# Writing the halves of q into the place of the loaded q, four buffers for split p, and new ranks for the planner

## The chip, the cores and the metric

The kernel runs on one core of one Trainium2 chip. The metric is the device time of one execution in microseconds (us), the median of several runs; lower is better.

## The reference, cut to what matters

Inputs: q, k and v of shape (4, 8, 1152, 64), w_in (512, 2048), w_out (2048, 512), all float32. The output is (2304, 512) float32.

```
q_pool = q.reshape(B, H, 576, 2, 64).mean(axis=3)
scores = q_pool @ k.T / sqrt(64); scores -= max(scores)
attn   = exp(scores);  attn /= sum(attn) + 1e-9
x      = heads side by side of (attn @ v)        # (4 * 576, 512)
h      = x @ w_in
out    = (h / (1 + exp(-1.702 * h))) @ w_out
```

## The kernel before, in words

**Stages.** The eight heads of a batch entry are taken two at a time, which gives 16 pairs (P = 0 to 15), four to a batch entry. A pair has nine tiles of 128 query rows against 1152 keys: four tiles of head A, four of head B, and a last one ("L") with 64 rows of each. So there are 144 tiles, numbered n. The feed-forward part follows per block of 256 tokens, nine blocks in all (72 steps of two 128-wide columns of h); a block can start once all four pairs of its batch entry are through, so it fills TensorE while later pairs are still in work, and the last blocks stand alone at the end.

**Two ways through attention.** Pairs 0 to 3 (36 tiles) are "whole": q, k and p stay float32 and are transposed on TensorE. Pairs 4 to 15 (108 tiles) are "split": each operand is written as a float16 high part and a float16 low part (the rest), and the float16 pieces are transposed by DMAs that SyncE (SP) issues.

**A tile of a split pair** passes these steps, each a function and a task of the planner: `scores` (six matmuls, line 675, into the one PSUM tile `s`), `row_max` on VectorE (DVE, line 689; writes `p`, three buffers, and so frees `s`), `lift` (lines 720 and 722, on DVE or ScalarE (ACT)), `exps` (ACT, line 696), `p_hi` (ACT or DVE, through `copy`, lines 258 and 260; writes the first half of `hl`, three buffers), `p_lo` (GpSimd (POOL) or DVE, line 730; writes the second half), `p_tr` (SP, line 743, a DMA transpose from `hl` into `pt`), and for every two tiles of A and two of B `pv` (line 756) with the reciprocals of the row sums (`w_denom` line 708, `w_recip` line 714, `w_rows` line 803). A buffer of `hl` comes free when its transpose has landed.

**Preparation of a pair.** `q_load` issues four DMAs on SP (lines 422 and 427) into `qraw`, which has one buffer. `q_add` (line 438, POOL but for pair 0) adds the two pooled rows into `qs`. For a split pair `q_max`, `k_max` and `v_max` (lines 444 and 453), `rows_max` on TensorE (line 465), `max_all` and `qkv_scale` give a power of two for each; `q_hi` (line 258) writes q's high part twice into columns 0 to 127 of `qn`, `q_lo` (line 505) its low part into columns 0 to 63 of the second half of `qn`; columns 64 to 127 of that half are zero for good, from one memset at the start (line 1128). `q_tr` (line 530) and `k_tr` (line 526) transpose `qn` and `kn` into `qT` and `kT`, two buffers each. `qn` is one constant tile of 128 x 2 x 9 x 128 float16, 4608 bytes in each partition; `qraw` (9 x 2 x 64 float32) has the same size.

**The feed-forward steps** are `moe_h` (line 978), `moe_tanh` (ACT, line 986), `moe_gate` (DVE, line 992), `moe_hi` (ACT, line 258, `g<-gf`), `moe_lo` (DVE, line 1003) and `moe_o` (line 1014).

**What sets the order.** A planner in Python (`Plan.order`) lays out all tasks before anything is issued. It goes through modelled time; of the tasks that could start soonest on an engine it takes the one with the lowest rank, a number built from the tile's n and the constants of `rank`. `movable` names the kinds of task that it may put on a second engine, `wait` how far past the earliest start it looks, `slack` stretches its costs, and `sizes` gives the number of buffers of each tile, both for the model and for the allocation. A task with `take=` holds a buffer until all tasks with `use=` of it are done. Each engine then runs its list strictly in that order, and waits with whatever is behind when a task's input or buffer is not there.

Of the kernel before, what the change touches and what calls it, by code (L numbers as in the profile page):

```python
# [11 lines left out]
F16 = mybir.dt.float16  # L12
# [129 lines left out]
def kernel(  # L142
# [26 lines left out]
    nc = tc.nc  # L169
    B, H, S, D = q.shape  # L170
# [4 lines left out]
    NJ = SQ // 64  # L175
# [9 lines left out]


    rank = dict(
        w1=1473.9738382899, w1_rate=812.7284009533, w2=2479.3934706835, w2_rate=62.2658245112,
        w1_cut=1764.9519973162, w1_cut_rate=0.0018904172, w2_cut=-269.851473856, w2_cut_rate=5.6062016033,
        v_max=1069.7920417805, load=-241.3418019351, prep=871.7951150424, max=-2026.5182514592,  # L190
        exp=640.8579795756, p_hi=-262.2674051923, p_lo=1525.5748408629, pv=1102.6265648828, x=557.4542312295,
        recip=1463.0570012603, w_tr=723.1050232894, w_ev=763.8780959185, g=-2229.8362745818,
        pv_b=-1120.3629115427, max_b=1656.4714364309, p_lo_b=1449.9352033366, prep_b=-1716.5596499645,
        v=1349.3135761977, lift=-444.2192073566,
    )
    movable = dict(DVE=('w_ev', 'x_hi', 'x_even', 'lift', 'qk_ev', 'p_hi', 'k_hi', 'v_hi'), POOL=('p_lo',))
    wait = dict(PE=0.010706, ACT=0.081524, DVE=0.106842, POOL=1.530524)
    slack = dict(PE=0.215686, ACT=1.104301, DVE=1.062313, POOL=1.096162, SP=1.036393, stay=30.678012)
    sizes = dict(
        qraw=1, qs=1, kraw=1, kn=1, qn=1, kT=2, qT=2, vraw=2, vhl=1,  # L200
        p=3, hl=3, pt=3, ptl=1, xt=2, xf=2, raw=4, th=2, gf=2, g=3, osb=2, s=1, tr=1, pv=1, h=1, o0=1, o1=1,
    )
    plan = Plan(sizes, wait, slack)
    const = ctx.enter_context(tc.tile_pool(name="const", bufs=1))
# [8 lines left out]
    wbuf = const.tile([128, 9, 2048], F32, name="wbuf")  # L213
    x16a = const.tile([128, 2, NP, 512], F16, name="x16a")
    xl = const.tile([128, NP, B, 64], F32, name="xl")
    qn = [const.tile([128, 2, NJ, 128], F16, name=f"qn{i}") for i in range(1)]
    s_qkv = const.tile([128, NPAIR, 3], F32, name="s_qkv")
    i_qkv = const.tile([128, NPAIR, 3], F32, name="i_qkv")
    e_s = const.tile([128, NPAIR], F32, name="e_s")
# [24 lines left out]
    def on(kind, **cost):  # L244
        return {e: c for e, c in cost.items() if kind in movable[e]}
# [4 lines left out]
    def dve(n, psum=False, fast=False):  # L250
        return n / (1920 if fast else 960) + (0.065 if psum else 0.068)
# [4 lines left out]
    def copy(e, out, in_, scale=None):  # L256
        if e == "ACT":
            nc.scalar.activation(out=out, in_=in_, func=ACTF.Copy, scale=1.0 if scale is None else scale)  # L258
        elif scale is None:
            nc.vector.tensor_copy(out=out, in_=in_)  # L260
        else:
            nc.vector.tensor_scalar(out=out, in0=in_, scalar1=scale, scalar2=None, op0=ALU.mult)
# [224 lines left out]
    def x_scale(b):  # L487
# [8 lines left out]
            in1=s_x[:, b:b + 1].to_broadcast([128, NP]), op=ALU.mult,  # L496
        )

    def q_hi(e, g):
        copy(e, qn[0][:, 0].rearrange("p j (c d) -> p j c d", c=2),  # L500
             T["qs", g.P].unsqueeze(2).to_broadcast([128, NJ, 2, D]), s_qkv[:, g.P, 0:1])

    def q_lo(g):
        t = qn[0]
        nc.vector.scalar_tensor_tensor(
            out=t[:, 1, :, 0:D], in0=T["qs", g.P], scalar=s_qkv[:, g.P, 0:1], in1=t[:, 0, :, 0:D],
            op0=ALU.mult, op1=ALU.subtract,
        )
# [18 lines left out]

    def q_tr(g):
        t = new("qT", ("qT", g.P), [128, 2 * NJ, 128], F16)
        nc.sync.dma_start_transpose(out=t, in_=qn[0].rearrange("p l j c -> p (l j c)"))  # L530

    PARTS = (("k", 0, 4), ("q", 0, 4), ("k", 4, 5), ("q", 8, 9), ("k", 5, 9), ("q", 4, 8))

# [46 lines left out]
    for g in pairs:  # L580
        n0, G = g.n0, g.P
        now = G == 0
        pe = ("DVE", nc.vector) if now else ("POOL", nc.gpsimd)
        gate = [] if n0 < 10 else [("E", n0 - 10)]
        r = n0 + rank["prep"] + (rank["prep_b"] if n0 >= 36 else 0.0)
        qr, qs, kr, kn, qk = ("qraw", G), ("qs", G), ("kraw", G), ("kn", G), ("qn", G)
        kt, qt = ("kT", G), ("qT", G)
        for i, what in enumerate("qkv"):
            key = (what + "raw", G)
            at, after = n0 + rank["load"] + 0.1 * i, [("E", n0 - 14 + i)] if n0 > 14 else []  # L590
            if what == "v" and g.wide:
                at, after = n0 + rank["v"] - 4, [("E", n0 - 5)] if n0 >= 5 else [("k_load", 0)]
            fn = dict(q=q_load, k=k_load, v=v_load)[what]
            plan.add(
                (what + "_load", G), "ACT" if what == "k" and not G else "SP", 2.1 if what == "q" else 0.8, at,
                lambda g=g, fn=fn: fn(g), after, take=[(what + "raw", key)], dma=2.0,
            )
        plan.add(("q_add", G), pe[0], dve(576) if now else gps(576), r, lambda g=g, e=pe[1]: q_add(g, e),
                 [("q_load", G)], take=[("qs", qs)], use=[qr], two=True)
        if g.wide:  # L600
            for i, (what, lo, hi) in enumerate(PARTS):
                pk = ("qkp", G, i)
                take = [(f"o{i % 2}", pk)] + ([("kT", kt)] if i == 0 else [("qT", qt)] if i == 1 else [])
                use = [qs if what == "q" else kr] + ([kt] if what == "k" and i else [qt] if what == "q" and i > 1 else [])
                plan.add(
                    ("qk_tr", G, i), "PE", 0.11 * (hi - lo), r - 20, lambda g=g, i=i: qk_tr(g, i),
                    [("q_add", G) if what == "q" else ("k_load", G)] + ([("qk_tr", G, i - 1)] if i else []),
                    take=take[:1], use=use[:1],
                )
                plan.add(  # L610
                    ("qk_ev", G, i), "ACT", act(128 * (hi - lo), True), r - 20, lambda e, g=g, i=i: qk_ev(e, g, i),
                    [("qk_tr", G, i)] + ([("qk_ev", G, i - 1)] if i else []), take=take[1:], use=[pk] + use[1:],
                    or_on=on("qk_ev", DVE=dve(128 * (hi - lo), True)),
                )
        else:
            plan.add(("q_max", G), "DVE", dve(576), r, lambda g=g: q_max(g), [("q_add", G)], use=[qs])
            plan.add(("k_max", G), "DVE", dve(1152), r, lambda g=g: kv_max(g, "k"), [("k_load", G), ("q_max", G)], use=[kr])
            maxima(g, r)
            plan.add(("q_hi", G), "ACT", act(1152, ptr=1), r, lambda e, g=g: q_hi(e, g), [("qkv_scale", G)],
                     take=[("qn", qk)], use=[qs], two=True, or_on=on("q_hi", DVE=dve(1152, fast=True)))  # L620
            plan.add(("q_lo", G), "DVE", dve(576) + 0.06, r, lambda g=g: q_lo(g), [("q_hi", G)], use=[qs, qk], two=True)
            plan.add(("k_hi", G), "ACT", act(1152, ptr=1), r, lambda e, g=g: k_hi(e, g), [("qkv_scale", G)],
                     take=[("kn", kn)], use=[kr], two=True, or_on=on("k_hi", DVE=dve(1152, fast=True)))
            plan.add(("k_lo", G), "DVE", dve(1152) + 0.06, r, lambda g=g: k_lo(g), [("k_hi", G)], use=[kr, kn], two=True)
            plan.add(("q_tr", G), "SP", 2.9, r, lambda g=g: q_tr(g), [("q_lo", G)], take=[("qT", qt)], use=[qk], dma=1.84, tr=True)
            plan.add(("k_tr", G), "SP", 2.9, r, lambda g=g: k_tr(g), [("k_lo", G)], take=[("kT", kt)], use=[kn], dma=1.84, tr=True)
        r = n0 + rank["v"]
        if g.wide:
            maxima(g, r + rank["v_max"])
        if g.whole:  # L630
            continue
        plan.add(("v_hi", G), "ACT", act(1152, ptr=1), r, lambda e, g=g: v_hi(e, g), [("qkv_scale", G)],
                 take=[("vhl", ("vhl", G))], use=[("vraw", G)], or_on=on("v_hi", DVE=dve(1152, fast=True)), two=True)
        plan.add(("v_lo", G), "DVE", dve(1152) + 0.06, r, lambda g=g: v_lo(g), [("v_hi", G)],
                 use=[("vraw", G), ("vhl", G)], two=True)
# [484 lines left out]
    with tc.manual_schedule():  # L1120
        make_identity(nc, idf)
        nc.vector.tensor_copy(out=idb, in_=idf)
        nc.vector.memset(ones, 1.0)
        nc.vector.memset(e_s, -1.0 / 16)
        for i, x in enumerate((LIFT * math.log(2.0), 1e-9, 1e-9 * 2 ** LIFT)):
            nc.vector.memset(add_c[:, i:i + 1], x)
        for t in qn:
            nc.gpsimd.memset(t[:, 1, :, D:], 0.0)
        for t, e in plan.order():
            t["fn"](e) if t["free"] else t["fn"]()  # L1130

# [29 lines left out]
```

## Time and profile before

| | |
|---|---|
| runs, us | 793.12, 797.49, 795.61; median 795.61 |
| the profiled execution | 796.71 us, span 795.0 us |
| busy share of the span | PE 95%, DVE 74%, ACT 72%, POOL 36% |
| mean granted TensorE clock | 0.997 |

PE is TensorE's matmuls, PEld its weight loads. In the split pairs' stretch the 16 DMA engines are busy throughout; at the end only PE is.

### The profile page before, as it was taken

The numbers are of one execution on the slowest core, as the hardware profiler recorded it, in microseconds if no ns is written. First come the engines' busy times: TensorE is split into PE (matmuls) and PEld (weight loads), VectorE is DVE, ScalarE is ACT, GpSimd is POOL, SyncE is SP. The second block draws the span as 40 slices with busy tenths as digits, with TensorE's granted clock in tenths as the row PEclk, the third lists the DMA queues.
The fourth block names the chain that finished last, engine by engine and source line by source line (L and its number), as shares of the span: only waits on it lengthen the run. The fifth ranks groups of instructions, "written<-read, shape, count | busy, mean of one in ns | idle before, by whom it ended". The sixth has DMA issues, their size and how long they took to land.

```text
span 795.0 us, 16660 instructions
## 1 busy us (share of the span) xinstructions
PE 754.4 (95%) x6716; PEld 509.3 (64%) x6716; DVE 584.7 (74%) x984; ACT 569.2 (72%) x929; POOL 286.0 (36%) x168
## 2 busy tenths in 40 slices
PE   5999999999998999999998998899999999999998
PEld 3565555656766677666675675666776677766664
DVE  5878999898887988788788887788787776222222
ACT  5988889789796878784777977776888886232322
POOL 3242242225746346334445543474364541000000
PEclk9999999999999999999999999999999999999999
DMA  9436073359999999999999999999999989010000
GB/s 302 171 136 217 30 247 112 113 120 189 208 206 202 189 225 185 215 201 214 180 209 217 208 179 196 236 205 200 194 226 187 173 127 177 1 28 2 27 1 26
DMA packets 335645, 128.75 MB, mean 162 GB/s; under 512 B 310736, under 2 KB 320976, under 8 KB 335568
## 3 DMA queue, kind: packets, MB, share of 16 engines
q1 hardware_dynamic: 335280, 127.10, 77.4%
q8 instruction: 52, 0.85, 0.4%
q10 hardware_dynamic: 288, 0.59, 0.3%
q14 instruction: 25, 0.20, 0.1%
HBM read 45.09 MB, written 4.72 MB: 63 GB/s over the span
## 4 chain that ended last, share of the span: by engine, by line
PE 61%; DMA 15%; DVE 10%; ACT 4%; issue 4%; POOL 3%; SPq 3%; POOLq 0%; DVEq 0%; ACTq 0%
PE h L978 16%; PE o L1014 15%; DMA pt<-hl 10%; PE s L675 7%; PE pv L756 7%; PE s L646 5%; DVE p L689 4%; PE o L768 4%; PE pv L791 4%; POOL hl L730 2%; ACT hl L258 2%; PE tr L803 2%; DMA raw<-in_moe_w_out_dram 1%; PE h L314 1%; SPq L743 1%
## 5 line engine op out<-in xcount | busy, mean ns | idle before, releaser
L730 POOL TENSOR_TENSOR hl<-p,hl 128x1152 f16<-128x1152 f32 x79 | 200.9, 2547 | 169.3 <-ACT hl L258 134.6
L689 DVE TENSOR_SCALAR_CACHE_REDUCE p<-s,e_s 128x1152 f32<-128x1152 f32 x144 | 203.3, 1412 | 34.5 <-PE s L675 24.0
L1014 PE MATMUL o<-wbuf,g 128*128 128x512 f16 x864 | 205.3, 379 | 1.2 <-DVE g L1003 1.2
L978 PEld LDWEIGHTS <-wbuf 128*128 128x128 f16 x1728 | 167.4, 98 | 41.9 <-issue 5.7
L696 ACT ACTIVATE p<-p,nm 128x1152 f32<-128x1152 f32 x144 | 179.8, 1249 | 12.5 <-DVE p L689 5.2
L258 ACT ACTIVATE hl<-p 128x1152 f16<-128x1152 f32 x99 | 114.4, 1157 | 43.3 <-DMA pt<-hl 41.6
L1014 PEld LDWEIGHTS <-g 128*128 128x128 f16 x864 | 83.2, 98 | 86.5 <-DVE g L1003 2.6
L675 PE MATMUL s<-kT,qT 128*128 128x384 f16 (+1 forms) x720 | 123.4, 326 | 10.3 <-DVE p L689 9.7
L978 PE MATMUL h<-x16a,wbuf 128*128 128x256 f16 x960 | 116.3, 273 | 0.7 <-DVE gf L992 0.7
L992 DVE SCALAR_TENSOR_TENSOR gf<-th,h 128x512 f32<-128x512 f32 x72 | 49.3, 684 | 83.7 <-ACT th L986 83.5
L986 ACT ACTIVATE th<-h,t_s 128x512 f32<-128x512 f32 x72 | 49.0, 680 | 77.8 <-PE h L978 77.0
L675 PEld LDWEIGHTS <-qT 128*128 128x128 f16 (+1 forms) x720 | 63.4, 100 | 54.1 <-issue 16.3
L978 PE MATMUL h<-wbuf 128*128 128x256 f16 x768 | 91.2, 273 | 2.7 <-DVE gf L992 2.7
L756 PEld LDWEIGHTS <-vhl 128*64 128x64 f16 x1944 | 83.7, 112 | 3.5 <-DMA pt<-hl 1.7
L756 PE MATMUL pv<-pt,vhl 128*64 128x256 f16 x1296 | 77.0, 276 | 2.5 <-DMA pt<-hl 2.5
L1003 DVE SCALAR_TENSOR_TENSOR g<-gf,g 128x512 f16<-128x512 f32 x72 | 62.3, 865 | 16.8 <-ACT g L258 16.6
L309 POOL TENSOR_TENSOR wbuf<-raw 128x512 f32<-128x512 f32 x32 | 35.4, 1115 | 82.7 <-ACT raw L305 82.7
L258 ACT ACTIVATE g<-gf 128x512 f16<-128x512 f32 x72 | 44.9, 623 | 22.0 <-DVE gf L992 22.0
L768 PE MATMUL o<-idf,p 128*128 128x128 f32 x324 | 49.2, 283 | 3.0 <-ACT pt L258 3.0
L646 PE MATMUL s<-kT,qT 64*128 64x512 f32 (+3 forms) x240 | 49.4, 523 | 1.5 <-DVE p L689 1.5
L730 DVE TENSOR_TENSOR hl<-p,hl 128x1152 f16<-128x1152 f32 x29 | 43.2, 1491 | 8.6 <-ACT hl L258 8.6
L768 PEld LDWEIGHTS o<-idf,p 128*128 128x128 f32 x324 | 35.2, 141 | 19.1 <-ACT pt L258 8.3
(105 smaller groups left out, 770.6 us busy)
## 6 DMA issues: line engine op xcount, KB each, us to landing
vraw<-in_v_dram SPq DMA_DIRECT2D x16, 576.0 KB, 5.1
kraw<-in_k_dram SPq DMA_DIRECT2D x15, 576.0 KB, 4.7
qraw<-in_q_dram SPq DMA_DIRECT2D x32, 256.0 KB, 3.5
raw<-in_moe_w_in_dram SPq DMA_DIRECT2D x16, 512.0 KB, 5.7
raw<-in_moe_w_out_dram SPq DMA_DIRECT2D x16, 512.0 KB, 4.9
out_dram<-osb SPq DMA_DIRECT2D x16, 256.0 KB, 2.6
pt<-hl SPq DMA_TRANSPOSE x96, 5.0
qraw<-in_q_dram SPq DMA_DIRECT2D x32, 32.0 KB, 3.3
```

The source lines that it names most:

```text
L258: nc.scalar.activation(out=out, in_=in_, func=ACTF.Copy, scale=1.0 if scale is None else scale)
L646: nc.tensor.matmul(out=ps[m, bank, 0:128 * (last - first)], lhsT=qT[h, (j - half) % NJ, m], rhs=kT[h, first:last].rearrange("p j c -> p (j ...
L675: nc.tensor.matmul(out=ps[m, c, 0:384], lhsT=st, rhs=T["kT", g.P][:, o:o + 3].rearrange("p r c -> p (r c)"), start=(l == 0), stop=(l == 1),)
L689: nc.vector.tensor_scalar(out=p, in0=s, scalar1=e_s[:, g.P:g.P + 1], scalar2=None, op0=ALU.mult, op1=ALU.min, accum_out=m)
L696: nc.scalar.activation(out=p, in_=p, func=ACTF.Exp, bias=T["nm", n], scale=-1.0, accum_out=sm)
L730: (nc.vector if e == "DVE" else nc.gpsimd).tensor_tensor(out=t[:, 1, :], in0=T["p", n].rearrange("p c f -> p (c f)"), in1=t[:, 0, :], op=A ...
L756: nc.tensor.matmul(out=ps[64 * a:64 * (a + 1), 0:w], lhsT=T["vhl", g.P][:, a, g.block[a][c], m], rhs=pt[:, l * KR + c, o:o + w], start=(pa ...
L768: nc.tensor.transpose(ps[:, 128 * i:128 * (i + 1)], T["p", n][:, c, 128 * i:128 * (i + 1)], idf)
L978: nc.tensor.matmul(out=h[:, e, :], lhsT=w1(2 * j + e, l, kk), rhs=x_rhs(blk, m, kk), start=(kk == 0 and l == 0 and m == 0), stop=(kk == KD ...
L992: nc.vector.scalar_tensor_tensor(out=gf, in0=T["th", blk, j], scalar=1.0, in1=T["h", blk, j].rearrange("p e n -> p (e n)"), op0=ALU.add, o ...
L1003: nc.vector.scalar_tensor_tensor(out=g[:, 1].rearrange("p e n -> p (e n)"), in0=T["gf", blk, j], scalar=2.0 ** -16, in1=g[:, 0].rearrange( ...
L1014: nc.tensor.matmul(out=o, lhsT=g[:, l, e, 128 * t:128 * (t + 1)], rhs=w2(fc, m), start=(fc == 0 and l == 0 and m == 0), stop=(fc == KFF - ...
```

## The change

Three things change together. First, the constant tile `qn` and its one memset go; q's halves are written into the memory of `qraw` of the same pair, read as float16 (`qn(g)`), after `q_add` has read the loaded values out of it. The zeros have to be written anew for each of the 12 split pairs, by a new POOL task `q_zero` after `q_add`. `qraw` (one buffer) is now held until `q_tr` has landed. Second, `hl` gets four buffers in place of three: 4608 bytes more in each partition, as many as `qn` took. Third, all constants of `rank`, `wait` and `slack` have new values, and DVE's list in `movable` changes: `moe_hi` and `x` (the task `w_spread`) may now go to DVE, `v_hi` no longer may; `w_sign` is named too, but that task has no second engine.

```diff
-        v=1349.3135761977, lift=-444.2192073566,
+        v=1408.7481183474, lift=-545.110055837,
...
-    movable = dict(DVE=('w_ev', 'x_hi', 'x_even', 'lift', 'qk_ev', 'p_hi', 'k_hi', 'v_hi'), POOL=('p_lo',))
-    wait = dict(PE=0.010706, ACT=0.081524, DVE=0.106842, POOL=1.530524)
-    slack = dict(PE=0.215686, ACT=1.104301, DVE=1.062313, POOL=1.096162, SP=1.036393, stay=30.678012)
+    movable = dict(DVE=('w_ev', 'qk_ev', 'k_hi', 'lift', 'p_hi', 'x', 'x_hi', 'x_even', 'moe_hi', 'w_sign'), POOL=('p_lo',))
+    wait = dict(PE=0.112533, ACT=0.093918, DVE=0.041114, POOL=1.05873)
+    slack = dict(PE=0.215686, ACT=1.140234, DVE=1.063168, POOL=1.225212, SP=1.031887, stay=39.737954)
     sizes = dict(
-        qraw=1, qs=1, kraw=1, kn=1, qn=1, kT=2, qT=2, vraw=2, vhl=1,
-        p=3, hl=3, pt=3, ...
+        qraw=1, qs=1, kraw=1, kn=1, kT=2, qT=2, vraw=2, vhl=1,
+        p=3, hl=4, pt=3, ...
-    qn = [const.tile([128, 2, NJ, 128], F16, name=f"qn{i}") for i in range(1)]
+    def qn(g):
+        t = T["qraw", g.P].rearrange("p j r d -> p (j r d)").bitcast(F16)
+        return t.rearrange("p (l j c) -> p l j c", l=2, c=128)
+
+    def q_zero(g):
+        nc.gpsimd.memset(qn(g)[:, 1, :, D:], 0.0)
...
             plan.add(("q_hi", G), "ACT", act(1152, ptr=1), r, lambda e, g=g: q_hi(e, g), [("qkv_scale", G)],
-                     take=[("qn", qk)], use=[qs], two=True, or_on=on("q_hi", DVE=dve(1152, fast=True)))
+                     use=[qs, qr], two=True, or_on=on("q_hi", DVE=dve(1152, fast=True)))
+            plan.add(("q_zero", G), "POOL", 0.58, r, lambda g=g: q_zero(g), [("q_add", G)], use=[qr])
-            plan.add(("q_tr", G), "SP", 2.9, r, ..., [("q_lo", G)], take=[("qT", qt)], use=[qk], dma=1.84, tr=True)
+            plan.add(("q_tr", G), "SP", 2.9, r, ..., [("q_lo", G), ("q_zero", G)], take=[("qT", qt)], use=[qr], dma=1.84, tr=True)
-        for t in qn:
-            nc.gpsimd.memset(t[:, 1, :, D:], 0.0)
```

Some ranks, before and after (a split pair's preparation counts from n0, its first tile; `BIG` tasks of the feed-forward matmuls are as before):

| | before | after |
|---|---|---|
| `prep` + `prep_b` (preparation of a split pair) | n0 - 845 | n0 - 987 |
| `max` + `max_b` (row_max of split tiles) | n - 370 | n - 283 |
| `p_hi` | n - 262 | n - 345 |
| `lift` | n - 444 | n - 545 |
| `pv` + `pv_b` (against n for `scores`) | n - 18 | n + 7 |
| `w2` (first of the second weight's 16 pieces) | 2479 | 2234 |
| `v` + `v_max` (v_max of whole pairs) | n0 + 2419 | n0 + 2413 |

## Rows read from the trace of the kernel before

**Rows 1.** The page, first part: busy us, share of the span, instructions.

```profile
PE 754.4 (95%) x6716; PEld 509.3 (64%) x6716; DVE 584.7 (74%) x984; ACT 569.2 (72%) x929; POOL 286.0 (36%) x168
```

**Rows 2.** Stretch; busy PE, PEld, DVE, ACT, POOL; granted clock, DMA share, GB/s.

```profile
0.00:20.00 20.00, 11.56 (x44) 6.52 (x45) 10.60 (x29) 10.57 (x17) 6.21 (x12) 1.00 0.91 303
20.00:180.00 160.00, 154.41 (x1163) 94.52 (x1162) 143.41 (x263) 137.34 (x261) 47.95 (x43) 1.00 0.45 142
180.00:662.00 482.00, 459.24 (x4566) 320.33 (x4563) 393.85 (x641) 381.92 (x592) 230.53 (x111) 1.00 1.07 199
662.00:791.30 129.30, 129.22 (x956) 87.96 (x952) 36.82 (x55) 38.75 (x62) 1.34 (x2) 1.00 0.12 26
```

**Rows 3.** Waits of TensorE, 180 to 662 us: total, times, longest us.

```profile
PE s L675 <- DVE p L689: 9.4, 11, 1.7
...
PE pv L756 <- DMA pt<-hl: 2.5, 2, 1.4
```

**Rows 4.** Waits of ScalarE, 180 to 662 us.

```profile
ACT hl L258 <- DMA pt<-hl: 41.6, 28, 5.7
```

**Rows 5.** Timeline: start, us, instruction, idle time before it and what ended it.

```profile
244.66 1.16 ACT L258 ACTIVATE hl<-p 128x1152 f16<-128x1152 f32 x1 [4.41 <-DMA pt<-hl]
246.28 0.66 PE L803 MATMUL tr<-idf,w_r 128*64 128x128 f32 x8 [2.65 <-DVE w_r L714]
...
339.00 1.16 ACT L258 ACTIVATE hl<-p 128x1152 f16<-128x1152 f32 x1 [3.05 <-DMA pt<-hl]
341.51 2.12 PE L978 MATMUL h<-wbuf 128*128 128x256 f16 x18 [1.61 <-DVE gf L992]
...
379.10 1.16 ACT L258 ACTIVATE hl<-p 128x1152 f16<-128x1152 f32 x1 [5.74 <-DMA pt<-hl]
381.62 2.14 PE L978 MATMUL h<-wbuf 128*128 128x256 f16 x18 [1.07 <-DVE gf L992]
...
418.78 1.16 ACT L258 ACTIVATE hl<-p 128x1152 f16<-128x1152 f32 x1 [3.77 <-DMA pt<-hl]
422.57 0.23 PE L465 MATMUL tr<-idb,qkv 128*128 128x128 bf16 x1 [1.46 <-DVE qkv L453]
...
612.10 0.76 DVE L260 CAST hl<-p 128x1152 f16<-128x1152 f32 x1 [2.61 <-DMA pt<-hl]
614.85 1.14 PE L675 MATMUL s<-kT,qT 128*128 128x384 f16 x6 [1.01 <-DVE p L689]
```

**Rows 6.** Timeline: the pv matmuls behind the longest gap, and later ones.

```profile
246.76 4.78 PE L756 MATMUL pv<-pt,vhl 128*64 128x256 f16 x54
...
602.89 3.12 PE L756 MATMUL pv<-pt,vhl 128*64 128x256 f16 x54
```

**Rows 7.** Transposes of p on SP: issuing time of one, ns min/median/max.

```profile
L743 SPq DMA_TRANSPOSE pt<-hl x96: 2403/2924/6049, 174.9 to 668.8; - x96
```

**Rows 8.** DMA issues, us from issue to landing: the transposes of q.

```profile
qT<-qn SPq DMA_TRANSPOSE x12, 5.0
```

**Rows 9.** Timeline: first q load of a pair and q transpose of the pair before.

```profile
187.11 0.58 SPq L422 DMA_DIRECT2D qraw<-in_q_dram  x1
...
199.39 2.62 SPq L530 DMA_TRANSPOSE qT<-qn  x1
...
472.72 3.85 SPq L530 DMA_TRANSPOSE qT<-qn  x1
...
489.44 0.57 SPq L422 DMA_DIRECT2D qraw<-in_q_dram  x1
```

**Rows 10.** The memset at the start: ns min/median/max.

```profile
L1128 POOL MEMSET qn<- x1: 577/577/577, 1.2 to 1.2; 128x576 f16 x1
```

**Rows 11.** Groups by line and form: count, busy us, mean ns, idle before.

```profile
L258 ACT ACTIVATE g<-gf 128x512 f16<-128x512 f32 x72 | 44.9, 623 | 22.0 <-DVE gf L992 22.0
...
L260 DVE CAST hl<-p 128x1152 f16<-128x1152 f32 x9 | 6.7, 754 | 5.1 <-DMA pt<-hl 3.9 <-ACT th L986 1.2
```

**Rows 12.** The same view, DVE from 180 to 662 us: the low part of g.

```profile
L1003 DVE SCALAR_TENSOR_TENSOR g<-gf,g 128x512 f16<-128x512 f32 x48 | 45.7, 952 | 0.2
```

More of the change, by code (lines that the diff above doesn't have):

```diff
@@ L187 @@
     rank = dict(
[L188 to L193, printed above, removed]
-        v=1349.3135761977, lift=-444.2192073566,
-    )
-    movable = dict(DVE=('w_ev', 'x_hi', 'x_even', 'lift', 'qk_ev', 'p_hi', 'k_hi', 'v_hi'), POOL=('p_lo',))
-    wait = dict(PE=0.010706, ACT=0.081524, DVE=0.106842, POOL=1.530524)
-    slack = dict(PE=0.215686, ACT=1.104301, DVE=1.062313, POOL=1.096162, SP=1.036393, stay=30.678012)
+        w1=1692.7092032715, w1_rate=0.0847319725, w2=2233.5160626376, w2_rate=94.8330985773,
+        w1_cut=1732.1541236565, w1_cut_rate=0.0043323258, w2_cut=-149.0274337882, w2_cut_rate=0.7748903456,
+        v_max=1004.6580165844, load=-255.3050973641, prep=703.1185782627, max=-2136.9316807791,
+        exp=1011.020352292, p_hi=-345.2989446467, p_lo=1626.1988371713, pv=1196.9974613641, x=411.6475496069,
+        recip=1864.3016783097, w_tr=666.680636295, w_ev=1060.0832994174, g=-2082.8137365706,
+        pv_b=-1189.8070304555, max_b=1853.9782174092, p_lo_b=1079.4294099435, prep_b=-1690.5236527256,
+        v=1408.7481183474, lift=-545.110055837,
+    )
+    movable = dict(DVE=('w_ev', 'qk_ev', 'k_hi', 'lift', 'p_hi', 'x', 'x_hi', 'x_even', 'moe_hi', 'w_sign'), POOL=('p_lo',))
+    wait = dict(PE=0.112533, ACT=0.093918, DVE=0.041114, POOL=1.05873)
+    slack = dict(PE=0.215686, ACT=1.140234, DVE=1.063168, POOL=1.225212, SP=1.031887, stay=39.737954)
     sizes = dict(
-        qraw=1, qs=1, kraw=1, kn=1, qn=1, kT=2, qT=2, vraw=2, vhl=1,
-        p=3, hl=3, pt=3, ptl=1, xt=2, xf=2, raw=4, th=2, gf=2, g=3, osb=2, s=1, tr=1, pv=1, h=1, o0=1, o1=1,
+        qraw=1, qs=1, kraw=1, kn=1, kT=2, qT=2, vraw=2, vhl=1,
+        p=3, hl=4, pt=3, ptl=1, xt=2, xf=2, raw=4, th=2, gf=2, g=3, osb=2, s=1, tr=1, pv=1, h=1, o0=1, o1=1,
     )
@@ L497, in x_scale @@
         )
+    def qn(g):
[3 more added lines that the diff above has]
+        nc.gpsimd.memset(qn(g)[:, 1, :, D:], 0.0)
     def q_hi(e, g):
-        copy(e, qn[0][:, 0].rearrange("p j (c d) -> p j c d", c=2),
+        copy(e, qn(g)[:, 0].rearrange("p j (c d) -> p j c d", c=2),
              T["qs", g.P].unsqueeze(2).to_broadcast([128, NJ, 2, D]), s_qkv[:, g.P, 0:1])
     def q_lo(g):
-        t = qn[0]
+        t = qn(g)
         nc.vector.scalar_tensor_tensor(
@@ L529, in q_tr @@
         t = new("qT", ("qT", g.P), [128, 2 * NJ, 128], F16)
-        nc.sync.dma_start_transpose(out=t, in_=qn[0].rearrange("p l j c -> p (l j c)"))
+        nc.sync.dma_start_transpose(out=t, in_=qn(g).rearrange("p l j c -> p (l j c)"))
     PARTS = (("k", 0, 4), ("q", 0, 4), ("k", 4, 5), ("q", 8, 9), ("k", 5, 9), ("q", 4, 8))
@@ L585 @@
         r = n0 + rank["prep"] + (rank["prep_b"] if n0 >= 36 else 0.0)
-        qr, qs, kr, kn, qk = ("qraw", G), ("qs", G), ("kraw", G), ("kn", G), ("qn", G)
+        qr, qs, kr, kn = ("qraw", G), ("qs", G), ("kraw", G), ("kn", G)
         kt, qt = ("kT", G), ("qT", G)
@@ L619 @@
             plan.add(("q_hi", G), "ACT", act(1152, ptr=1), r, lambda e, g=g: q_hi(e, g), [("qkv_scale", G)],
-                     take=[("qn", qk)], use=[qs], two=True, or_on=on("q_hi", DVE=dve(1152, fast=True)))
-            plan.add(("q_lo", G), "DVE", dve(576) + 0.06, r, lambda g=g: q_lo(g), [("q_hi", G)], use=[qs, qk], two=True)
+                     use=[qs, qr], two=True, or_on=on("q_hi", DVE=dve(1152, fast=True)))
+            plan.add(("q_lo", G), "DVE", dve(576) + 0.06, r, lambda g=g: q_lo(g), [("q_hi", G)], use=[qs, qr], two=True)
+            plan.add(("q_zero", G), "POOL", 0.58, r, lambda g=g: q_zero(g), [("q_add", G)], use=[qr])
             plan.add(("k_hi", G), "ACT", act(1152, ptr=1), r, lambda e, g=g: k_hi(e, g), [("qkv_scale", G)],
@@ L624 @@
             plan.add(("k_lo", G), "DVE", dve(1152) + 0.06, r, lambda g=g: k_lo(g), [("k_hi", G)], use=[kr, kn], two=True)
-            plan.add(("q_tr", G), "SP", 2.9, r, lambda g=g: q_tr(g), [("q_lo", G)], take=[("qT", qt)], use=[qk], dma=1.84, tr=True)
+            plan.add(("q_tr", G), "SP", 2.9, r, lambda g=g: q_tr(g), [("q_lo", G), ("q_zero", G)], take=[("qT", qt)], use=[qr], dma=1.84, tr=True)
             plan.add(("k_tr", G), "SP", 2.9, r, lambda g=g: k_tr(g), [("k_lo", G)], take=[("kT", kt)], use=[kn], dma=1.84, tr=True)
```

## The prediction, made before the changed kernel had run

> **What bounds the kernel now.** I read the busy shares first. TensorE's matmuls are busy for 754.4 us of a span of 795.0 [rows 1], so PE has 40.6 us without a matmul, and nothing in the change adds or removes a matmul. Any gain must come out of those 40.6 us. The view by stretch [rows 2] says where they lie: 8.4 us in the first 20 us, 5.6 in the whole pairs (160.00 - 154.41), 22.8 in the split pairs (482.00 - 459.24), 0.1 while the feed-forward stands alone, and the 3.7 us after 791.3 in which only the last rows are stored. Start and store are out of the change's reach; what it can move is 22.8 plus 5.6 us.
>
> Next I took the waits of TensorE in the split pairs [rows 3]. Its largest item, 9.4 us in 11 waits, is `scores` waiting until `row_max` has emptied `s`; 2.5 us are `pv` waiting for a transposed p. These name the engine that was last, not the cause. So I went to the waits of ScalarE: `p_hi` stood 28 times, 41.6 us in all, in front of an `hl` buffer that a transpose had not yet given back [rows 4]. While it stands, everything behind it on ACT stands too: tanh, `q_hi`, the reciprocals' sums. The timeline shows such a stop and then PE empty [rows 5]: ACT free at 244.66 after 4.41 us, PE idle 2.65 us until the reciprocals of the same tile come; 3.05 us, then PE idle 1.61 (tanh, gate, then h); 5.74, then 1.07; 3.77, then 1.46 (by way of `v_max`, which had waited on DVE behind a gate); and once with `p_hi` on DVE, 2.61, then 1.01. Five stops, 2.65 + 1.61 + 1.07 + 1.46 + 1.01 = 7.80 us of PE.
>
> The first had a sequel. The granted clock was at its lower level (1.2 GHz) for a few us just behind the gap, and the `pv` part that ran there took 4.78 us where the same 54 matmuls take 3.12 elsewhere [rows 6]: 1.66 us more. It is the only such dip after the start. With it, stops for `hl` cost PE 7.80 + 1.66 = 9.46 us.
>
> **The change, part by part.**
>
> *Four buffers for `hl`.* With four, `p_hi` of tile n waits for the transpose of tile n-4 and not n-3. Transposes in a row follow each other by their issuing time on SP, 2.92 us in the median [rows 7], so each stop gets shorter by about that: 4.41, 3.05, 5.74 and 3.77 leave 1.49, 0.13, 2.82 and 0.85, and 2.61 leaves nothing. Since 2.92 (or 2.61) is longer than each PE gap behind it, all five gaps and the dip could go: -9.46 us is the far end. The near end is 0 and not a gain: the buffer makes no transpose faster. The kernel has 108 transposes of p and 24 of q and k; at 2.92 us each (an estimate for the few kinds without a row) that is 385 us of SP's 482, and the DMA engines show a share of 1.07 in this stretch [rows 2]. What is late next, then, is the transposed p itself, which `pv` already awaits for 2.5 us [rows 3]. Between the ends I take half: -4.73 us. It is the half because the stops come in bursts of transposes, where a fourth buffer helps once and then is full as well.
>
> *q's halves in `qraw`'s place.* The values written, the number of instructions and their shapes for `q_hi`, `q_lo` and `q_tr` stay. What changes is that the four load DMAs of the next pair's q must stand behind the landing of this pair's `q_tr`. The transpose lands 5.0 us after issue [rows 8]. Late in the kernel `q_tr` is issued at 472.72 and the next load at 489.44 [rows 9]: 16.7 - 5.0 = 11.7 us to spare, and eight of the eleven changes of pair are like this (15 to 19 us from issue to load). Near the switch from whole to split pairs it's the other way round: the load at 187.11 comes 12.3 us ahead of the `q_tr` at 199.39, so it must move by 12.3 + 5.0 = 17.3 us; one pair earlier the same. What it feeds there is not urgent: the pair that is loaded at 187.11 has its first `scores` some 60 us later. So 0 us, from 0 to a stop of PE at each change of pair, which I price below as a rival. If SP carries the load ahead of ready transposes, its wait holds up all of them.
>
> *The zeros.* 12 memsets on POOL at 0.577 us [rows 10], 6.9 us, in place of one. POOL is busy 230.5 of 482 us there [rows 2], and DVE and ACT, not POOL, stand last before PE. Cost 0; at most 6.9 us if POOL's cover were gone altogether, and no gain, since the old memset ran once at the start.
>
> *Ranks, wait, slack and movable.* This reorders all engines, and no row shows the new order. In the whole pairs the gain can't exceed PE's 5.6 us. The loss there: DVE is busy 143.4 of 160 us, and where `row_max` was late PE lost 9.4/11 = 0.85 us each time; one in four of 36 tiles would be +7.7 us. In the split pairs the order of kinds on DVE stays nearly as it was (`p_hi` now ahead of `row_max`), and on PE `scores` comes ahead of a ready `pv`, which empties `s` into `p` sooner. `moe_hi` on DVE would spare ACT 0.623 us a step and cost DVE about 0.754 x 512/1152 = 0.34 [rows 11]. I take 0, as no row leans either way, and keep -5.6 and +7.7.
>
> Sum: -4.73 + 0 + 0 + 0. The profiled execution took 796.71 us (span 795.0 and 1.7 around it), which gives 791.98; it was 1.1 us above the median of the runs, 795.61, so on the median's scale I predict **790.9 us**.
>
> **The rivals.**
>
> *The wait only moves.* `p_hi` goes on sooner, fills the fourth buffer, and PE meets the same queue of transposes at `pv`. For it: 385 of 482 us of issuing, DMA share 1.07. Against it: `pv` waited for p only twice. Time: 795.6, give or take 3 for the new order.
>
> *More than half.* All gaps behind `hl` go (-9.46) and the new order closes half of the 5.6 us in the whole pairs: 795.6 - 9.5 - 2.8 = 783. For it: every stop's shortening exceeds the gap behind it. Against it: two of the four longest stops keep over 1 us.
>
> *The q load becomes a block on SP (slower).* If the new order prepares a pair so late that `q_tr` lands after the next load's place, SP stands in front of that load with ready transposes behind it. It decides once preparation moves by more than 11.7 us against the loads. Price: where a missing p stopped `pv`, PE lost 2.5/2 = 1.25 us; at half of 11 changes of pair 6.9 us, and without the buffer's gain 802.5. Against it: preparation goes from n0 - 845 to n0 - 987 in rank, so it keeps its place ahead.
>
> *DVE becomes the limit (slower).* If all 48 steps of this stretch have `moe_hi` on DVE, that is 0.34 x 48 = 16 us; if each also ran as late as `moe_lo` does here, 0.952 us against about 0.69 elsewhere ((72 x 0.865 - 48 x 0.952)/24, from the page's mean of 0.865 for all 72) [rows 12], 29 us. DVE's room falls from 88 to 59 us, and the 9.4 us of waits for `row_max`, scaled by 88/59, become 14.0: +4.6, so 800. The Trainium skill has the rule behind it (SBUF — State Buffer, "Who interferes with whom"): a copy or tensor_scalar in a two-port mode on VectorE and an instruction on GpSimd lock each other out for a whole instruction, while ScalarE waits for nobody. By that rule the moved `moe_hi` would be held by `p_lo` on POOL; the slow `moe_lo` agrees with it for two-input instructions, and no row here shows it for `moe_hi`.
>
> **How the numbers follow.** Forecast 0.42 (own range 786 to 794); the wait moves 0.25; more than half 0.13; the block on SP 0.11; DVE 0.09. From 795.61 a run can be told from no change at about 0.5%, 4 us: below 791.6 or above 799.6. Faster: 0.37 of the forecast's 0.42, all of the 0.13, 0.02 of the moving wait, 0.52. Slower: 0.03 of the moving wait, 0.10 of the block and 0.06 of DVE, 0.19. The rest, 0.29, is the same. The range runs from 781 (795.6 - 9.5 - 5.6 is 780.5) to 802, just short of the block's own value; it leaves about 0.2 out.
>
> **What would show it.** In the changed kernel's waits of ScalarE, `hl` behind a transpose should fall from 41.6 us to 20 or less, and no `pv` part should take 4.8 us. PE's busy time should stay at 754 and its gap in the split pairs come down to about 18 us. POOL should show 12 memsets of 0.58 us, with nothing waiting for them. The loads of q should follow `q_tr` by more than 5 us with no stop of SP. It is wrong if SP waits on a q load, if `pv`'s waits for p grow by as much as ACT's shrink, or if the gap of the whole pairs, which I left alone, changes by more than 3 us.

## The result: 1.1% slower, and the profile after

The changed kernel takes 805.07 us (803.47 to 805.46) against 795.54 us: a ratio of 1.0114, 95% interval 1.0093 to 1.0134. The prediction was 790.9 us, range 781 to 802: wrong in sign and outside the range.

The busy shares of the changed kernel, and its stretches (start and end, busy us of PE, PEld, DVE, ACT and POOL with counts, clock, DMA share, GB/s):

```profile
PE 757.2 (94%) x6716; PEld 509.9 (63%) x6716; DVE 586.2 (73%) x1011; ACT 559.7 (70%) x896; POOL 309.3 (38%) x185
```

```profile
0.00:20.00 20.00, 11.14 (x45) 6.36 (x47) 10.13 (x26) 10.12 (x18) 5.48 (x11) 1.00 0.90 298
20.00:180.00 160.00, 153.28 (x1127) 93.62 (x1126) 141.33 (x266) 139.50 (x254) 48.07 (x46) 1.00 0.43 139
180.00:672.00 492.00, 464.86 (x4640) 323.92 (x4638) 399.86 (x670) 374.73 (x573) 255.12 (x128) 1.00 1.06 200
672.00:800.00 128.00, 127.93 (x911) 85.95 (x908) 34.84 (x52) 34.67 (x54) 0.67 (x1) 1.00 0.04 13
```

Against [rows 1, 2], the span grew by 8.6 us (795.0 to 803.6): PE is busy 2.8 us longer and idle 5.8 us longer (803.6 - 757.2 = 46.4, before 40.6). Of the idle time 0.4 us came at the start, 1.1 in the whole pairs and 4.4 in the split pairs (27.1 against 22.8). The last of the stretches starts at 672 us here and at 662 before, but the split pairs end no later: their last `pv` matmul starts at 678.3 us, before at 678.1. What PE lost until then is left over as feed-forward matmuls, and what stands behind that `pv` takes 8.4 us longer (125.3 against 116.9).

Where TensorE waits in that stretch of the changed kernel (total us, times, longest), and the lines of the kernel before in the same view that [rows 3] left out:

```profile
PE s L682 <- DVE p L696: 10.6, 13, 2.8
PE pv L763 <- DMA pt<-hl: 10.3, 8, 2.1
PE pv L763 <- DMA ptl<-hl: 1.5, 1, 1.5
PE h L985 <- DVE gf L999: 1.3, 2, 0.7
...
PE tr L464 <- DVE qkv L452: 0.9, 2, 0.6
...
PE tr L816 <- DVE w_r L721: 0.3, 1, 0.3
```

```profile
PE h L978 <- DVE gf L992: 3.3, 3, 1.6
PE tr L465 <- DVE qkv L453: 2.9, 3, 1.5
PE tr L803 <- DVE w_r L714: 2.7, 1, 2.7
```

The three waits through which stops for `hl` had reached PE fell from 8.9 to 2.5 us: -6.4, near the size foretold, though not by the way foretold, as ScalarE's own stops below show. But `pv` waits 11.8 us for transposed p where it waited 2.5: +9.3. With +1.2 at `scores` that makes +4.1 of the 4.4. The idle gain was spent again, and more, at `pv`. PE's longer busy time lies there too. The group of the `pv` matmuls (count, busy us, mean ns, idle before) in the kernel before, and in the changed one:

```profile
L756 PE MATMUL pv<-pt,vhl 128*64 128x256 f16 x1296 | 77.0, 276 | 2.5 <-DMA pt<-hl 2.5
```

```profile
L763 PE MATMUL pv<-pt,vhl 128*64 128x256 f16 x1296 | 79.7, 277 | 10.4 <-DMA pt<-hl 10.3
```

That is 2.7 of the 2.8 us. Part of it is the broken start: at six of the waits one matmul runs alone (0.27 us) and the other 53 take 3.11 us or more, where 54 in a row take 3.12 [rows 6].

ScalarE's waits for `hl` in the changed kernel hardly moved from [rows 4]:

```profile
ACT hl L257 <- DMA pt<-hl: 37.8, 21, 3.9
```

One such stop in the timeline of the changed kernel: `pv` issues one matmul and then stands until its second transpose has landed. Behind the gap the granted clock falls, as it did in [rows 6], to 0.50 from 336 to 338 us (its lower level, 1.2 GHz), and 53 matmuls take 4.80 us.

```profile
332.74 0.27 PE L763 MATMUL pv<-pt,vhl 128*64 128x256 f16 x1
...
335.03 4.80 PE L763 MATMUL pv<-pt,vhl 128*64 128x256 f16 x53 [2.01 <-DMA pt<-hl]
```

### The profile page after: what moved, and what is told of

It reads as the page before. It is cut to its first block, busy times and chain, and to the rows that moved or that the text cites. A ratio compares the mean times of both kernels' runs of the same rounds, so it can differ in the third digit from the quotient of the medians.

```text
span 803.6 us, 16728 instructions
## 1 busy us (share of the span) xinstructions
PE 757.2 (94%) x6716; PEld 509.9 (63%) x6716; DVE 586.2 (73%) x1011; ACT 559.7 (70%) x896; POOL 309.3 (38%) x185
## 4 chain that ended last, share of the span: by engine, by line
PE 55%; DVE 16%; DMA 14%; issue 5%; ACT 3%; SPq 3%; POOL 3%; DVEq 0%; POOLq 0%; ACTq 0%
PE h L985 14%; PE o L1021 13%; DMA pt<-hl 8%; PE s L682 6%; PE pv L763 6%; DVE p L696 6%; PE s L653 4%; PE pv L798 4%; PE o L775 3%; DMA qraw<-in_q_dram 3%; POOL hl L737 2%; SPq L750 2%; PE h L313 1%; DMA vraw<-in_v_dram 1%; SPq L426 1%
## 5 line engine op out<-in xcount | busy, mean ns | idle before, releaser
L737 POOL TENSOR_TENSOR hl<-p,hl 128x1152 f16<-128x1152 f32 x85 | 219.1, 2581 | 152.8 <-ACT hl L257 83.5
L257 ACT ACTIVATE hl<-p 128x1152 f16<-128x1152 f32 x91 | 105.3, 1158 | 42.8 <-DMA pt<-hl 37.8
L682 PE MATMUL s<-kT,qT 128*128 128x384 f16 (+1 forms) x720 | 123.4, 327 | 10.6 <-DVE p L696 10.6
L763 PEld LDWEIGHTS <-vhl 128*64 128x64 f16 x1944 | 84.1, 112 | 15.9 <-DMA pt<-hl 8.0
L763 PE MATMUL pv<-pt,vhl 128*64 128x256 f16 x1296 | 79.7, 277 | 10.4 <-DMA pt<-hl 10.3
L1010 DVE SCALAR_TENSOR_TENSOR g<-gf,g 128x512 f16<-128x512 f32 x72 | 57.1, 795 | 18.9 <-ACT g L257 18.8
L257 ACT ACTIVATE g<-gf 128x512 f16<-128x512 f32 x60 | 37.4, 623 | 27.1 <-DVE gf L999 27.0
L437 POOL TENSOR_TENSOR qs<-qraw 128x576 f32<-128x576 f32 (+1 forms) x18 | 23.2, 1296 | 59.6 <-DMA qraw<-in_q_dram 45.3
```

Of the source, the lines that this page charges most:

```text
L682: nc.tensor.matmul(out=ps[m, c, 0:384], lhsT=st, rhs=T["kT", g.P][:, o:o + 3].rearrange("p r c -> p (r c)"), start=(l == 0), stop=(l == 1),)
L737: (nc.vector if e == "DVE" else nc.gpsimd).tensor_tensor(out=t[:, 1, :], in0=T["p", n].rearrange("p c f -> p (c f)"), in1=t[:, 0, :], op=A ...
L763: nc.tensor.matmul(out=ps[64 * a:64 * (a + 1), 0:w], lhsT=T["vhl", g.P][:, a, g.block[a][c], m], rhs=pt[:, l * KR + c, o:o + w], start=(pa ...
L1010: nc.vector.scalar_tensor_tensor(out=g[:, 1].rearrange("p e n -> p (e n)"), in0=T["gf", blk, j], scalar=2.0 ** -16, in1=g[:, 0].rearrange( ...
```

## The experiments

Ratios are to the kernel before, run on the same chip in the same session, with 95% intervals. Unless said otherwise "new order" is the changed kernel's.

### The parts one by one: e1 to e4

**e1, the buffer without a new order.** The planner keeps three `hl` buffers in its model and gives the old order; memory has four.

```diff
-    plan = Plan(sizes, wait, slack)
+    plan = Plan(dict(sizes), wait, slack)
+    sizes['hl'], sizes['th'] = 4, 3
...
-    w_r = const.tile([128, NJ * NPAIR], F32, name="w_r")
+    w_r = w_d
...
-        gf = new("gf", ("gf", blk, j), [128, 512], F32, moe_pool())
+        gf = T["gf", blk, j] = T["th", blk, j]
```

> The kernel before, laid out by the planner as before (three hl buffers in its model, old ranks, qn a tile of its own), but with a fourth hl buffer really there; the room comes from writing gate's result over th's and the reciprocals over the row sums, which adds no wait in this order. The prediction's term for the buffer alone: ACT's waits for hl fall from 41.6 us to 20 or less and the time to about 791 (-4.7). Rival (the wait only moves to pv): ACT's waits fall but PE waits more for transposed p, time 795 within 2. Third theory (the buffer does harm by itself): slower, 799 or more.

Measured: 0.9956 (0.9921 to 0.9991), 793.23 against 797.87 us. Its group of `p_hi` on ACT (count, busy us, mean ns, idle before) and its PE waits:

```profile
L259 ACT ACTIVATE hl<-p 128x1152 f16<-128x1152 f32 x99 | 114.1, 1153 | 2.0 <-DMA pt<-hl 1.2
```

```profile
PE s L676 <- DVE p L690: 7.7, 10, 1.7
...
PE pv L757 <- DMA pt<-hl: 5.4, 7, 2.8
```

ACT's wait fell from 41.6 to 1.2 us, and part of it came back as `pv` waiting 5.4 us in place of 2.5. The term of the sum (-4.7) holds: 0.44% of 796 is 3.5 us, 0.7 to 6.3. This version is faster than both kernels.

**e2, the same buffer told to the planner**, with old ranks and the room made as in e1.

```diff
-        p=3, hl=3, pt=3, ...
+        p=3, hl=4, pt=3, ...
```

> The kernel before with four hl buffers in the planner's model as well as in memory, old ranks, qn a tile of its own. If the order that the planner makes of four buffers does the harm (it sends p_hi ahead, and pv then waits on PE for transposes the model lands too early), about 800 to 805 and PE's waits of pv for transposed p near 10 us. If the ranks do it, about 791 to 796 and pv waits near 2.5 us.

Measured: 1.0295 (1.0278 to 1.0312). The harm is there, but not where I expected it: `pv` waits for nothing, and `scores` wait for `row_max`.

```profile
PE s L676 <- DVE p L690: 22.9, 16, 3.8
```

**e3, the new constants alone** (rank, movable, wait and slack of the change on the kernel before).

```diff
-        w1=1473.9738382899, w1_rate=812.7284009533, ...
+        w1=1692.7092032715, w1_rate=0.0847319725, ...
...
-    wait = dict(PE=0.010706, ACT=0.081524, DVE=0.106842, POOL=1.530524)
+    wait = dict(PE=0.112533, ACT=0.093918, DVE=0.041114, POOL=1.05873)
...
```

> The kernel before with the new rank, wait, slack and movable alone; three hl buffers, qn a tile of its own. Theory that the new order costs it: 803 or more, with PE's waits of pv for transposed p well above the 2.5 us of before. Theory that the structure costs it: 795 within 3.

Measured: 1.0459 (1.0435 to 1.0483), `scores` waiting 35.2 us and `pv` 9.1.

**e4, the new structure with the old constants** (the change without its new rank, movable, wait and slack).

> The changed kernel (q's halves in qraw, zeros anew for each pair, four hl buffers) with the old rank, wait, slack and movable. Theory that the new ranks cost it: 791 to 796. Theory that the structure costs it: 803 or more, like the changed kernel, with q loads or pv waiting.

Measured: 1.0166 (1.0136 to 1.0196), `scores` waiting 21.9 us and `pv` 7.5. So neither theory of e3 and e4 stands alone: with the new structure the new constants are better than the old (1.0114 against 1.0166), on the old structure they are far worse (1.0459 against 1). In these runs a set of constants belongs to one configuration.

### Is it the buffer or q's place in the new order: e5, e6

**e5**, the new order with a fifth buffer that the planner doesn't know:

```diff
+    plan = Plan(dict(sizes), wait, slack)
+    sizes['hl'], sizes['th'] = 5, 3
```

> The changed kernel in its own order (planned with four hl buffers), with a fifth hl buffer that the planner does not know; the room as in e1. Theory that a buffer helps only where it is spare beyond the plan: ACT's waits for hl fall from about 40 us to under 5 and the time by 3 to 8 us against the changed kernel's 805, to about 799 to 802. Rival (the plan's order has its loss elsewhere, and no spare buffer changes it): 803 to 806.

Measured: 1.0114 (1.0086 to 1.0142): no gain. ScalarE's and TensorE's waits in e5:

```profile
ACT hl L258 <- DMA pt<-hl: 0.4, 1, 0.4
```

```profile
PE pv L764 <- DMA pt<-hl: 14.9, 12, 2.5
...
PE pv L764 <- DMA ptl<-hl: 1.6, 1, 1.6
```

ACT no longer waits, and `pv` waits 16.5 us in place of 11.8. My theory that a spare buffer always pays fell here.

**e6**, the new order with q's halves in a tile of their own again (its room made as in e1):

```diff
     def qn(g):
-        t = T["qraw", g.P].rearrange("p j r d -> p (j r d)").bitcast(F16)
-        return t.rearrange("p (l j c) -> p l j c", l=2, c=128)
+        return qn0
```

> The changed kernel in its own order, but q's halves are written into a tile of their own again (each pair's zeros are still written), so that no q load has to wait for a transpose of q. Theory that q's place costs nothing by itself: 805 within 2, the changed kernel's time. Rival (the load behind the transpose is part of the loss): 801 or less.

Measured: 1.0121 (1.0099 to 1.0143). In this order, q's place costs nothing by itself; that the planner counted on it when it made the order is another matter (e18).

### Is any other order as bad: e7, e8

**e7** and **e8** change one constant of the kernel before each:

```diff
-    slack = dict(PE=0.215686, ACT=1.104301, DVE=1.062313, POOL=1.096162, ...
+    slack = dict(PE=0.215686, ACT=1.104301, DVE=1.062313, POOL=1.10, ...      # e7
+    slack = dict(PE=0.215686, ACT=1.106, DVE=1.062313, POOL=1.096162, ...     # e8
```

> The kernel before with one constant of the planner changed, POOL's slack 1.096162 to 1.10 (0.35%): three hl buffers, qn of its own, old ranks. The planner's order differs from tile 2 on. Theory that any new order costs, because the constants fit one order and the planner's model doesn't see what the chip does: 803 or more. Theory that only the change's own constants or buffers are bad: 796 within 4.

> The kernel before with ACT's slack 1.104301 to 1.106 (0.15%), nothing else; the order is the old one up to tile 73 and differs from there. Theory that any new order costs: 800 or more, about half of what e7 loses, all of it after 300 us. Theory that only the change's own constants or buffers are bad: 796 within 4.

Measured: e7 1.0185 (1.0158 to 1.0212), `scores` waiting 15.9 us for `row_max`; e8 1.0009 (0.9985 to 1.0033). A change of 0.35% in one constant, which the chip never sees but through the order, costs more than the whole change under study; another is free. So an order made anew can be worse than the old one for next to no reason in the kernel, but need not be.

### Would pv be better off later: e9 to e11, e14, e15

**e9 to e11** exchange each split pair's `pv` with the next tasks on TensorE, where inputs and buffers allow, after the planner is done.

```diff
-        for t, e in plan.order():
+        for t, e in later_pv(plan, plan.order(), 2):
```

> The changed kernel; in its order each pv of a split pair (w_rows and the three parts) goes behind up to two of the next other tasks on TensorE, where no task's inputs or buffers forbid it (59 exchanges over 36 pv); every other engine's list is as it was. Theory that the changed kernel loses its time where pv stands at the head of TensorE for a p that is not transposed: PE's waits of pv for hl's transposes fall from 11.8 us to under 4 and the time from 805 to 797 within 2.5. Rival (TensorE waits there for something that is late anyway, and the wait turns up at scores or h): 803 or more with PE's waits for row_max up.

> e5 (the changed kernel's order with a fifth hl buffer that the planner does not know) with the same exchanges of pv as in e9. In e5 the fifth buffer took ACT's waits for hl away and the waits of pv grew from 11.8 to 16.5 us with the time unchanged. If pv's place on TensorE is what ate that gain, the buffer pays now: below e9 by 2 to 5 us, 792 to 796. If not, the same as e9.

> e1 (old order, a fourth hl buffer that the planner does not know) with pv later in the same way (68 exchanges). In e1 pv waited 5.4 us for transposes, against 2.5 before. If those waits are a loss like the changed kernel's, they fall under 2 us and the time to 0.99 of before or less (about 790 against 797). Rival: pv later holds pt buffers longer and delays x, so that 0.995 stays or is lost.

Measured: e9 1.0643 (1.0596 to 1.0690), e10 1.0661 (1.0596 to 1.0727), e11 1.0466 (1.0419 to 1.0512). In all three the first theory missed and the rival came true, by far more than I had expected. In e9 `pv` waits for nothing; two lines of its waits say why that is no use:

```profile
PE s L738 <- DVE p L752: 49.8, 33, 5.0
...
DVE xf L896 <- PE pv L819: 49.6, 17, 6.2
```

DVE's list has `x` where `pv` used to end, so DVE now stands there, `row_max` behind it, and the next `scores` behind `row_max`.

**e14, e15** move only the second `pv` of a pair, and only behind feed-forward tasks:

```diff
+    for name in [n for n in seqs["PE"] if n[0] == "pv" and n[1] >= first and n[2:] == (1, 0)]:
...
+            j = next(j for j in range(i + 1, len(q)) if q[j][0] in "ho")
```

> The changed kernel; only the second pv of each split pair (u = 1, where seven of the nine waits of pv stand) goes behind the next two feed-forward tasks of TensorE (24 exchanges, 1.3 us of cover each), and scores keep their place before or after it but for that. Theory that the waits of pv are time lost: the waits fall from 11.8 to about 4 us and the time to about 799. Rival as in e9 (the tile's scores and x are as urgent as pv, so anything that holds pv back costs as much): 805 or more, DVE waiting on pv for x.

> e1 with the same exchange. If the 5.4 us of pv waits in e1 are time lost, 789 to 791 against e1's 0.9956 of before. Rival: 0.996 or worse.

Measured: e14 1.0140 (1.0089 to 1.0191), e15 1.0026 (1.0001 to 1.0052) where e1 had 0.9956. In e15 `pv` waits 1.8 us in place of 5.4, and `scores` 14.0 in place of 7.7. In e14 the wait was only in part taken away: `pv` still waits 9.1 us (11.8 in the changed kernel) and `scores` 14.2 (10.6). The rival holds where `pv` was freed (e9 to e11, e15): its wait could not be scheduled away on TensorE alone, because what depends on it was as urgent. In e14 that was hardly put to the test.

### Transposes that come sooner: e12, e13

Both orders, with half of p's transposing left out:

```diff
-        src = T["hl", n].rearrange("p l f -> p (l f)")
+        src = T["hl", n].rearrange("p l f -> p (l f)")[:, S // 2:S // 2 + S]
...
-        nc.sync.dma_start_transpose(out=d, in_=src)
+        nc.sync.dma_start_transpose(out=d[:, 0:KR], in_=src)
...
-                    rhs=pt[:, l * KR + c, o:o + w], ...
+                    rhs=pt[:, c, o:o + w], ...
```

> The changed kernel in its order, but each transpose of p carries only half of hl (the second half of the high part and the first half of the low), and pv reads these blocks for all its terms: half of p's transposing is left out, so its output is not the reference's. Theory that the new order loses its time to transposes that come late: with p there sooner, waits of pv and of p_hi for transposes near 0 and the time within 4 us of e13. Rival (the new order loses elsewhere, and the pv waits only stand in its place): still 8 to 12 us above e13.

> The kernel before with the same half of p's transposing left out. ACT's waits for hl should go (41.6 us before) and PE's 9.5 us behind them: 786 to 789. It is the yardstick for e12.

Measured: e12 781.82 us, 0.9819 (0.9773 to 0.9866); e13 781.68 us, 0.9820 (0.9772 to 0.9868). The 9.5 us between the two orders are gone; e13 itself came out 4 us below its expectation. The issuing time of a transpose on SP (ns min/median/max) in e12 and then e13; it was 2924 in [rows 7]:

```profile
L750 SPq DMA_TRANSPOSE pt<-hl x96: 1257/1314/4528, 177.8 to 642.6; - x96
```

```profile
L743 SPq DMA_TRANSPOSE pt<-hl x96: 1242/1303/3898, 175.0 to 652.8; - x96
```

Neither has a wait of `pv` or `p_hi` for a transpose. The new order lost 23 us' worth of lateness, the old one 14. These two runs show that the loss comes by way of p's transposes: in the new order they come late for those who need them, by more than in the old. They don't say what makes them late, since half the transposing also leaves SP and the DMA engines freer for everything else that they carry.

### Who makes them late: e16 to e18

**e16, e17** shorten the step in front of the transpose on GpSimd, in both orders:

```diff
+        if e == "POOL":
+            nc.gpsimd.tensor_scalar(
+                out=t[:, 1, :].bitcast(F32), in0=t[:, 0, :].bitcast(F32), scalar1=0.0, scalar2=1.0, ...
```

> The changed kernel in its order; where GpSimd makes the low part of p it only writes zeros there, from the high part read as 576 float32 (about half the time of its subtraction), so p's low part is left out in those tiles and the output is not the reference's. Transposes are whole. Theory that in the new order the transposes come late because GpSimd hands them over late (SP waited for it 81 us against 60): the gap to e17 closes to under 4 us. Rival (the transposes and loads on SP and the DMA engines are what is late, whoever hands over): the gap stays at 7 us or more, with pv still waiting 8 us or more.

> The kernel before with the same short p_lo on GpSimd; the yardstick for e16. By the first theory of e16 it gains less than e16 does, 790 to 794; by the rival both gain the same, if anything.

Measured: e16 1.0017 (0.9997 to 1.0037), e17 0.9871 (0.9832 to 0.9910). TensorE's waits of `pv` in e16, and in e17:

```profile
PE pv L769 <- DMA pt<-hl: 10.4, 10, 1.9
...
PE pv L769 <- DMA ptl<-hl: 2.1, 2, 1.7
```

```profile
PE pv L762 <- DMA pt<-hl: 2.8, 2, 1.8
```

Both orders gain about 1%, the gap between them stays (798.17 against 787.58), and so do the waits, 12.5 and 2.8 us. GpSimd's length isn't the difference between the orders. The time of the hand-over is not settled by it: SP still waits 89.7 us for GpSimd's half of `hl` in e16 (81.1 in the changed kernel) and 60.8 in e17 (60.2 before).

**e18**, the new structure, old constants, and a fourth buffer that the planner doesn't know (e4 told it):

```diff
+    plan = Plan(dict(sizes), wait, slack)      # hl=3 in its model
+    sizes['hl'] = 4
```

> q's halves in qraw, old ranks, and the planner told of three hl buffers while four are there (e4, 811, told it of four). Holding q in qraw makes the planner give another order from pair 5 on. Theory that the old ranks fit one order only: 800 to 815 again. Theory that the planner's use of the fourth buffer was e4's loss: 792 to 796, like e1.

Measured: 1.0107 (1.0072 to 1.0143), 805.57 us, inside the first expectation. Telling the planner cost e4 another 0.6%, but the larger part, 1.0107 against e1's 0.9956, comes with the order that the planner makes of the new structure from pair 5 on. The structure is two things for the planner, q's hold on `qraw` and the 12 new tasks of the zeros; which of them turns the order was not separated on the chip.

## Why the prediction was wrong, point by point

**What bounds the kernel** was read rightly: no matmul came or went, and 5.8 of the 8.6 us lie in PE's gaps, the rest in longer `pv` matmuls.

**Four buffers for `hl`** was right as a cause and as a size where nothing else changed: -4.7 foretold, -3.5 (-0.7 to -6.3) in e1. In the changed kernel it was wrong to keep it. The stops that I had traced did leave PE (8.9 to 2.5 us), but ACT's waits stayed at 37.8 us where I foretold 20 or less, because the planner was told of the buffer and laid `p_hi` out to use it: where it wasn't told, these waits were 1.2 us (e1) and 0.4 (e5). So the waits of PE that fell did so with the new order and not by the shorter stops that I had summed.

**q's halves in `qraw`'s place** was right at 0 for the wait itself: e6 without it takes the same time. The loads follow the issue of `q_tr` by 5.7 us or more, after 120 us SP has no wait at the lines of a q load, and near [rows 9]'s first pair the load moved behind the transpose:

```profile
199.60 2.74 SPq L536 DMA_TRANSPOSE qT<-qraw  x1
...
206.58 0.54 SPq L421 DMA_DIRECT2D qraw<-in_q_dram  x1
```

What I didn't price is that a `qraw` held longer, and the zeros' tasks, change the planner's order (e18).

**The zeros** cost nothing by their length that can be seen: 12 memsets, in the median at the time of [rows 10], and GpSimd shortened by far more than their 6.9 us leaves the gap between the orders as it was (e16, e17). I had foretold that nothing would wait for them; the view of SP's waits puts 19.3 us, in 6 waits before transposes of p, down to the memset, and what part of these it caused is not shown.

```profile
L503 POOL MEMSET qraw<- x12: 578/578/1076, 140.0 to 577.8; 128x576 f16 x12
```

**The step that failed is the 0 for the new order.** It stands in "Ranks, wait, slack and movable ... I take 0", with +7.7 as its far end, and in the "So 0 us" for q's place, which priced the wait of a load and not the order. The new order against the old one with a spare fourth buffer is 1.0114 / 0.9956 = 1.0159, +12.6 us. It can't be booked to the constants alone, for the terms don't add: with the old constants the new structure costs as much (e18 against e1, 1.0107 / 0.9956), on the structure of e4 the new constants gain about 0.5%, and on the old structure they lose 4.6% (e3).

It failed in three ways. The bound was drawn from the whole pairs and from `row_max`, whose waits changed by 1.2 us; the loss came in the split pairs at `pv`, 9.3 us of idle time behind transposes and 2.7 us of busy time. And 0 was the wrong middle: of the orders made anew here without help by hand (after, e2, e3, e4, e7, e8, e18), six were 1.1 to 4.6% slower and one the same, none faster. The old order was a lucky or chosen one. Third, "no row shows the new order" passed over what the planner itself says. Its modelled end (`self.span` in `Plan.order`, Python that needs no chip) is 776.2 us for the kernel before and 780.6 for the changed one; for e8, e18, e7, e4, e2 and e3 it is 778.0, 787.7, 789.8, 794.4, 804.5 and 823.4. The slack constants are part of the model, so e3, e7, e8 and the changed kernel are not measured with quite the same rule; still, each of the six slower orders is slower in the model, the differences to before within 11 us of the measured ones.

**Its signs of being wrong** were well chosen: `pv`'s waits grew by 9.3 us while ACT's for `hl` shrank by 3.8, one `pv` part took 4.80 us, and the gap of the split pairs went to 27.1 us and not to 18.

**The rivals.** "The wait only moves" named the mechanism, `p_hi` ahead and `pv` in front of the same queue of transposes, but took it to be worth no more than the gain. "The block on SP" and "DVE becomes the limit" did not happen: SP did not stand in front of a q load in the split pairs, DVE is busy 73% against 74%, and `moe_hi` went to DVE in 12 of the 72 steps (at 437 ns each, where I had put 340).

**Open**: what in the new order makes transposes late. They are not slower: 2.92 us of issuing in the median in both kernels, 5.3 us to landing against 5.0. It isn't q's place (e6), a lack of `hl` buffers (e5), GpSimd's length (e16 against e17) or `pv`'s place on TensorE alone (e9). But the trace shows which of them are late. Between 180 and 660 us 24 transposes of p in either kernel stand on SP directly behind a load of the next pair's q, k or v, and such a one holds SP for 4.0 us in the median (3.1 to 6.0). In the changed kernel `pv` waited for 7 of these 24, which is 7 of its 8 waits for `pt`; before, for 2 of the 24, which is both of its waits. The one that ended the gap of 2.01 us above (the 6.02 us):

```profile
323.93 0.53 SPq L421 DMA_DIRECT2D qraw<-in_q_dram  x1
...
326.34 0.47 SPq L409 DMA_DIRECT2D kraw<-in_k_dram  x1
326.91 6.02 SPq L750 DMA_TRANSPOSE pt<-hl  x1
333.03 0.53 SPq L557 DMA_DIRECT2D vraw<-in_v_dram  x1
```

So in the new order `pv` stands more often for a transpose behind a load. No run moved the loads, so whether that order of transposes and loads on SP or the bunching of tiles ahead of it is the cause was not separated.

## What to carry to other kernels

When a change lets a planner lay everything out anew, price the new order as a term of its own: run the planner and compare its modelled end before and after, and don't put the mean at zero without a reason; test the resource alone by giving it to the memory and not to the planner. A wait that ends at one place in a static order says who was last, not that moving the waiting task helps: its dependents stand on other engines' lists at the old place. To find out whether two orders differ by one resource, make that resource faster in both and see whether they meet.

## What the runs showed of the hardware

DVE's busy time fell with no change to its own instructions when GpSimd's step was shortened: 584.7 us before, 567.8 in e17, where GpSimd's `p_lo` takes 774 ns (2547 before). `moe_lo`, with two inputs, went from 865 to 720 ns in the mean; `row_max` stayed at 1412. Halving the transposed bytes more than halved SP's issuing time of a transpose, 2.92 to 1.30 us, and took its time from issue to landing from 5.0 to 3.1 us in the old order and from 5.3 to 3.4 in the new. A transpose of p directly behind a load on SP held SP for 4.0 us in the median, against 2.92 for all.

The granted clock fell to 0.50 behind the gap of 2.01 us before the `pv` at 335.03 in the changed kernel, and stayed at 1.00 behind one of 2.06 us before the `pv` at 377.77. In e2, e3 and e9, with a mean granted clock of 0.980, 0.982 and 0.978 against 0.997, PE was busy 764.0, 762.6 and 771.8 us for the same 6716 matmuls that took 754.4 before.
